# Later scatters, one block of scores and the first tile's rows taken forward, and a third 512-column first layer, in a fused attention and expert kernel

## The chip, the core and the metric

The kernel runs on one core of a Trainium2 chip, on five engines: TensorE (PE), whose weight loads are shown apart as PEld, VectorE (DVE), ScalarE (ACT), GpSimd (POOL) and SyncE (SP). SP and POOL issue DMA transfers. The metric is the device time of one launch in microseconds (us), the median of three runs; lower is better.

## The reference

Two layers follow one another. The first is a linear attention with a decay for each head, over 4 batches, 8 heads, 768 tokens and 64 channels; it goes through the tokens in blocks and carries a state of 64 by 64 per head.

```python
for b in range(nb):
    intra = np.einsum('bhic,bhjc->bhij', qb, kb) * Dmask[None]
    intra = np.einsum('bhij,bhjd->bhid', intra, vb)
    inter = np.einsum('bhid,bhde->bhie', qb * lam_pow[None], kv_state)
    out[:, :, sl] = intra + inter
    kv_state = lam_block[None, :, None, None] * kv_state + np.einsum('bhsd,bhse->bhde', kb_dec, vb)
```

Its output, 3072 tokens of 512 numbers, goes into a mixture of 8 experts. A token takes the one expert with the largest logit, and the expert is two layers of 512 by 1024 and 1024 by 512 with a ReLU between them.

```python
logits = x @ w_gate + modality_bias[modality_id]
e_idx = np.argmax(logits, axis=1)
for e in range(E):
    mask = e_idx == e
    h = np.maximum(x[mask] @ w1[e], 0.0)
    out[mask] = gate_w[mask, None] * (h @ w2[e])
```

## The kernel before

**Attention.** Tokens are taken in 24 blocks of 128 (`g` in the code), six to a batch, two to a step `m` (0 to 11). A block has scores (`scores`, L261, PE into the PSUM tile `s`, two buffers), the decay mask on DVE (`mask`, L267, into `pt`), decayed keys on ACT (`keys`, L243), decayed queries on POOL (`query`, L228, `qd`), the products that make the state (`products`, L275, PE into the single PSUM tile `kv`), the state's sum on DVE (`add`, L286), what comes from the state (`from_state`, L309) and from the block itself (`values`, L319), both PE into the PSUM tile `o` (two buffers), and a copy `xt` out of PSUM (`give`, L298). `block(g)` is scores, mask, keys and query. The loop over `m` works one step ahead: step m issues the blocks 2m+2 and 2m+3, then takes `from_state` and `values` of 2m and 2m+1, then the products of the next two.

**Rows.** After each odd step, `turns` turns four finished blocks from columns into rows by transposes on PE (`turn`, L338, into `o`), with the gate's logits between them (`gates`, L356). DVE (L345) and ACT (L348) copy each turned block from `o` into the rows `grp`.

**Routing.** Blocks are routed in three batches of 8. Small DVE operations work out a slot for each token; they are queued by `put` and issued a few at a time by `do(n)`. POOL then writes the rows to the DRAM tensor `placed`, block by block, with an indirect DMA (`one_slot`, L442 and L443). These scatters wait in a list of jobs; `tick(mm)` takes the next of them and lets it wait for the matmul mm. Those of the first batch go out in steps 5 to 7. A list of tiles is made of the counts: `early_list` "A" names the first two tiles of 256 tokens of one expert, "B" the next two, `late_list` the rest.

**Experts.** All products are made of float32 numbers split in a high part in fp32r and a low part, and a product is high by high, high by low and low by high. `fetch_x(n)` has SP fetch a tile's rows from `placed` (`xg`, four transfers of 128 KB, L629) and its tags (`idx`), after reading the place from a list by a register load; `fetch_w1` (`raw1`, L681) and `fetch_w2` (`raw2`, L685) fetch the weights in four parts of 512 KB. `turn_rows` transposes the rows on DVE in two halves (`turned`, L690, into `xt2`); `split_rows` and `split_w1` cast to high parts on ACT (L610, `xhl`, `w1h`) and subtract on DVE (L611, `xhl`, `w1l`); `low_w1` (L915) is such a subtraction for the first tile, into `low`. The first layer comes in two forms. `first_layer` makes three matmuls of 256 columns per piece (`three`, L702 to L704) into `s` and `kv` in turn, then a ReLU on ACT (`hh`, L725) and the low part on DVE (`hl`, L726). `first_joined` makes one matmul of 512 columns (high weights by high and low rows side by side, L742) and one of 256 (L741, L745) into `s`; then ACT copies one half (`hb`, L749), DVE adds the halves (`hs`, L751), ACT makes `hh` (L752) and DVE `hl` (L754). `second(n, t)` is the second layer of half a tile: 24 matmuls of 512 columns, a scaled copy on ACT (`y`, L769) and an indirect DMA on POOL to the output (L770). Before the change tiles 0 and 2 use `first_layer`, tile 1 and all from 3 on `first_joined`.

**Order.** PE, DVE, ACT and SP run in the order in which the code issues; POOL's order is made by dependencies that `pool` adds, which comes to the order of the code as well. So a transpose that waits for rows holds up all that DVE has behind it, and a fetch that waits holds up SP's later fetches. The attention's last steps, m = 9 to 11, overlap the first tile's preparation: in step 10 DVE turns the first tile's rows, and in step 11 it makes `xhl` and `low`. When the rows of tile 3 have been used, SP clears the end of each expert's region in `placed` (`clear_end`, eight transfers), then fetches w1 and the rows of `wides`, the fifth full tile (number 6 in the list).

Of the kernel before, what the change touches and what calls it, by code (L numbers as in the profile page):

```python
# [15 lines left out]
P = 128  # L16
# [27 lines left out]
def linear_attention_moe(tc, qkv, lam, modality, wg, mbias, w1, w2, out):  # L44
    nc = tc.nc
    with ExitStack() as ctx:
# [199 lines left out]
        scs = {}  # L246
# [110 lines left out]
                                          start=(p == 0), stop=(p == NP - 1), tile_position=(0, t * Q))  # L357
            return mm

        def turns(grp, amid):  # L360
            turn(grp, 0)
            turn(grp, 1)
            mm = gates(grp)
            do(4)
            amid()
            turn(grp, 2)
            return mm, turn(grp, 3)

        shape = [P, RC, E]

# [11 lines left out]
        def do(n=None):  # L382
            for what, args, kw in todo[:n]:
                what(*args, **kw)
            del todo[:n]
# [302 lines left out]
        def turned(out, rows):  # L688

            return nc.vector.transpose(out=out.rearrange("q p (t a) -> q t p a", a=Q),  # L690
                                       in_=rows.rearrange("q t (p a) -> q t p a", a=Q))

        def turn_rows(n):
            for h in range(2):
                turned(xt2[:, :, h * P : (h + 1) * P], xgs[n][:, 4 * h : 4 * (h + 1), :])

        def split_rows():
            for i in range(2):
# [126 lines left out]
        xgs = {}  # L825
# [30 lines left out]

        pairs = B * NC // HB
        def block(g, on_pool=False):
            mm = scores(g)
            mask(g)  # L860
            keys(g, on_pool)
            query(g)
            return mm
# [62 lines left out]
        for m in range(2, pairs):  # L926
            a, b = HB * m, HB * m + 1
            ahead = m + 1 < pairs
            add(b)
            if m == 4 or m == 8:  # L930
                routed = m // 4 - 1, *choose(m // 4 - 1, gate_rows())
            if ahead:
                block(a + 2)
                mm = block(b + 2)
                if m > 4:
                    tick(mm)
                if 2 < m <= pairs - SLOTS:
                    after(load(m + SLOTS - 1, [1]), mm)
                if m == 9:
                    fetch_w1(*some, parts=range(2, 4))  # L940
                elif m == 10:
                    fetch_w2(*some, parts=range(2, 4))
# [3 lines left out]
            if m == 10:  # L946
                w1h = w1_part("w1h", F32R, True)
                w1l0 = [work.tile([P, KC, TT], F32R, name="low", tag=f"both{i}" if i < 4 else "dk", bufs=1) for i in range(1, 5)]
                nc.scalar.copy(out=w1h[0], in_=raw1[0])
                do(4)  # L950
                turn_rows(0)
            elif not ahead:
                split_rows()
                low_w1(0)
                split(raw1[1], w1h[1], w1l0[1])
                do(4)
            elif m == 2:
                routing_constants()
            elif m == 3:
                clear(slice(E * CAP, E * CAP + TT), TT)  # L960
# [12 lines left out]
                mm = values(b)  # L973
            if m == 4 or m == 8:
                do(1)
            if m > 4:
                tick(mm)
            if m + SLOTS < pairs:
                load(m + SLOTS, [0])
            if ahead:  # L980
                mm = products(a + 2)
                mm = products(b + 2) or mm
                if m == 7:
                    tick(mm)
                add(a + 2)
            if m % 2 and ahead:
                ends = turns(m // 2, begin_list)
                if m == 5 or m == 9:
                    jobs += [("slots", one_slot)] * RC
                for mm in ends[: 2 if m % 4 == 1 else 1] if m > 4 else ():  # L990
                    tick(mm)
            if m == 8:
                need("slots")
# [74 lines left out]
            second(1, t)  # L1068
        need("slots")

        first_layer(amid2)
        fetch_w2(*fetch_regs(3))
        turn_rows(3)
        split_rows()
# [1 line left out]
        for e in range(E):  # L1076
            clear_end(e)
        do()
        fetch_w1(*fetch_regs(wides, True))
        fetch_x(wides)  # L1080
        for t in range(2):
            second(2, t)

# [114 lines left out]
```

## Time and profile before

| what | us |
|---|---|
| median of three runs | 383.61 |
| lowest and highest run | 383.05, 384.69 |
| the profiled execution, its own time | 384.85 |
| its span, first to last instruction | 383.1 |
| PE busy | 373.5 (97% of the span) |
| DVE busy | 282.9 (74%) |
| ACT busy | 237.4 (62%) |
| POOL busy | 99.0 (26%) |

The granted clock of TensorE was 0.997 over the span. Busy time of PE includes the overlap of neighbouring matmuls, whose ends are modelled: a stretch without idle time is a stretch in which starts follow each other, and the pace is read from the distance of starts, not from the length of one. An engine's idle time in brackets stands before an instruction, with what ended it. Times in the timelines are from the span's start.

### The profile page before, as it was taken

Reading aid. Unit: us, or ns where it says so; the run is one execution under the profiler, and the core shown is the slowest. Engines: PE = TensorE matmul, PEld = TensorE weight load, DVE = VectorE, ACT = ScalarE, POOL = GpSimd, SP = SyncE. Lnnn points to the kernel's source line nnn. Section 1 sums busy time; section 2 is a strip of 40 time slices with the busy share of each in tenths; the row PEclk is TensorE's granted clock in tenths of the full one; section 3 lists DMA queues with packets and bytes.
Section 4 is the critical chain, followed back from the end, with each engine's and each line's share of the span. In section 5 each row is a group of like instructions: output and inputs, shape, how many; then the busy total and the mean of one; then the engine's idle time right before and its main releaser. Section 6 shows DMA issues by size and latency. Waiting matters only on the chain.

```text
span 383.1 us, 9168 instructions
## 1 busy us (share of the span) xinstructions
PE 373.5 (97%) x3316; PEld 318.1 (83%) x3316; DVE 282.9 (74%) x506; ACT 237.4 (62%) x458; POOL 99.0 (26%) x130
## 2 busy tenths in 40 slices
PE   8999999999999999999999999999999999999993
PEld 3889989888998889888888877788878888888882
DVE  6677978779777889867789584486876868688630
ACT  1577676777766765564766664456566665776621
POOL 3653238628600177020100102102011020201112
PEclk9999999999999999999999999999999999999998
DMA  7999988999979684599714899763870210300100
GB/s 246 386 408 385 363 315 282 394 294 354 295 255 292 230 232 180 220 347 326 208 52 122 268 409 313 285 191 91 290 233 30 56 55 19 93 0 3 55 29 27
DMA packets 44597, 82.69 MB, mean 216 GB/s; under 512 B 7406, under 2 KB 20222, under 8 KB 44544
## 3 DMA queue, kind: packets, MB, share of 16 engines
q1 hardware_dynamic: 40592, 69.23, 55.6%
q0 software_dynamic: 3952, 12.79, 8.8%
q8 instruction: 28, 0.46, 0.5%
q14 instruction: 25, 0.20, 0.2%
HBM read 89.52 MB, written 17.85 MB: 280 GB/s over the span
## 4 chain that ended last, share of the span: by engine, by line
PE 56%; issue 33%; POOL 5%; DVE 3%; DMA 2%; SPq 0%; POOLq 0%; ACT 0%; DVEq 0%
PE s L742 8%; PE o L702 6%; PE o L704 6%; PE o L703 6%; PE s L261 6%; PE o L319 5%; POOL out_dram L770 4%; PE o L338 3%; PE s L741 3%; PE o L309 3%; PE kv L275 2%; DMA load<-in_qkv_dram 2%; PE x L356 1%; PE s L704 1%; PE kv L702 1%
## 5 line engine op out<-in xcount | busy, mean ns | idle before, releaser
L742 PE MATMUL s<-xhl,w1h 128*128 128x512 f32 x320 | 108.2, 395 | 0.0
L770 POOL DMA_INDIRECT out_dram<-y,idx x24 | 28.7, 1198 | 213.1 <-ACT y L769 167.8
L702 PE MATMUL o<-w2h,hh 128*128 128x512 f32 x192 | 75.1, 391 | 0.0
L703 PE MATMUL o<-w2l,hh 128*128 128x512 f32 x192 | 74.8, 389 | 0.0
L704 PE MATMUL o<-w2h,hl 128*128 128x512 f32 x192 | 74.7, 389 | 0.0
L741 PE MATMUL s<-xhl,w1l 128*128 128x256 f32 x240 | 67.2, 280 | 0.0
L742 PEld LDWEIGHTS s<-xhl,w1h 128*128 128x128 f32 x320 | 55.2, 188 | 7.7 <-issue 0.4
L751 DVE TENSOR_TENSOR hs<-s,hb 128x512 f32<-128x512 f32 x40 | 27.6, 690 | 43.8 <-ACT hb L749 43.8
L611 DVE TENSOR_TENSOR w1l<-raw,w1h 128x1024 fp32r<-128x1024 f32 x44 | 51.7, 1220 | 2.0 <-ACT w1h L610 2.0
L753 DVE TENSOR_TENSOR w2l<-raw,w2h 128x1024 fp32r<-128x1024 f32 x40 | 48.6, 1215 | 0.0
L741 PEld LDWEIGHTS s<-xhl,w1l 128*128 128x128 f32 x240 | 45.1, 188 | 3.6
L610 ACT CAST w1h<-raw 128x1024 fp32r<-128x1024 f32 x47 | 46.0, 1045 | 0.0
L752 ACT ACTIVATE hh<-hs 128x512 fp32r<-128x512 f32 x40 | 25.3, 633 | 30.7 <-DVE hs L751 29.9
L702 PEld LDWEIGHTS o<-w2h,hh 128*128 128x128 f32 x192 | 36.0, 188 | 7.8 <-issue 0.8
L704 PEld LDWEIGHTS o<-w2h,hl 128*128 128x128 f32 x192 | 36.0, 188 | 7.6
L703 PEld LDWEIGHTS o<-w2l,hh 128*128 128x128 f32 x192 | 36.1, 188 | 7.3
L735 ACT CAST w2h<-raw 128x1024 fp32r<-128x1024 f32 x40 | 41.5, 1038 | 0.0
L243 ACT ACTIVATE kd<-load,dk 128x64 f32<-128x64 f32 x144 | 35.7, 336 | 2.4 <-DMA load<-in_qkv_dram 2.3
L610 ACT CAST xhl<-xt 128x512 fp32r<-128x512 f32 x24 | 13.7, 619 | 30.9 <-DVE xt L690 29.7
L443 POOL DMA_INDIRECT placed<-grp,sloti x24 | 26.7, 1114 | 20.5 <-PE o L338 8.2
L228 POOL TENSOR_TENSOR qd<-load,pq 128x512 f32<-128x512 f32 x20 | 25.3, 1280 | 24.5 <-PE s L261 20.2
L267 DVE TENSOR_TENSOR pt<-s,dk 128x1024 f32<-128x1024 f32 x24 | 28.5, 1213 | 3.0 <-PE s L261 2.9
(209 smaller groups left out, 584.9 us busy)
## 6 DMA issues: line engine op xcount, KB each, us to landing
raw<-in_w_dram SPq DMA_DIRECT2D x96, 512.0 KB
load<-in_qkv_dram SPq DMA_DIRECT2D x12, 1024.0 KB
both<-in_w_dram SPq DMA_DIRECT2D x16, 512.0 KB
xg<-placed SPq DMA_DIRECT2D x48, 128.0 KB
placed<-blank SPq DMA_DIRECT2D x9, 528.0 KB
load<-in_qkv_dram SPq DMA_DIRECT2D x8, 512.0 KB
load<-in_qkv_dram SPq DMA_DIRECT2D x2, 2048.0 KB
load<-in_qkv_dram SPq DMA_DIRECT2D x4, 768.0 KB
```

The lines of the kernel that those rows point to most:

```text
L243: nc.scalar.activation(out=kds[g][:, p, hl, :], in_=kn[:, p, hl, :], func=AF.Copy, scale=dk[:, hl, p, P - 1 : P])
L267: nc.vector.tensor_tensor(out=pts[g], in0=scs.pop(g), in1=dk, op=ALU.mult)
L610: nc.scalar.copy(out=hi, in_=src)
L611: nc.vector.tensor_tensor(out=lo, in0=src, in1=hi.bitcast(F32), op=ALU.subtract)
L702: nc.tensor.matmul(out, ah, bh, start=first, stop=False)
L703: nc.tensor.matmul(out, ah, bl, start=False, stop=False)
L704: return nc.tensor.matmul(out, al, bh, start=False, stop=last)
L735: nc.scalar.copy(out=w2h[i], in_=raw2[i])
L741: nc.tensor.matmul(hp[:, j, :TT], w1l[i][:, kc, fs], xh[c][:, d, :], start=False, stop=False)
L742: mm = nc.tensor.matmul(hp[:, j, :], w1h[i][:, kc, fs], xhl[c][:, d].rearrange("p h t -> p (h t)"), start=(kc == 0), stop=(kc == KC - 1))
L753: nc.vector.tensor_tensor(out=w2l[i], in0=raw2[i], in1=w2h[i].bitcast(F32), op=ALU.subtract)
L770: sc = nc.gpsimd.indirect_dma_start(out=out, out_offset=bass.IndirectOffsetOnAxis(ap=idx[:, t, 0:1], axis=0), in_=y, in_offset=None, bound ...
```

## The change

Five things change. (1) The scatters of the first batch go out by other ticks: step 6 releases one (after its products) where it released two, step 7 one after the scores of block 16, one after the products and two after the turns, and the eighth is left to step 8, after the scores of block 19. (2) The scores of block 18 are issued in step 7 ahead of `turns`, and not at the head of step 8. (3) The first tile's rows are turned in step 9, a half between `gates` and the third turn and a half after the fourth, and not in step 10; in step 10 the state's sum of block 21 comes after the masks of blocks 22 and 23, `low_w1(0)` is issued there, and the four first operations of list B go from step 10 to step 11, behind the other part of `low`. (4) Tile 2's first layer is `first_joined`. (5) The rows of `wides` are fetched ahead of its w1.

```diff
--- before.py
+++ after.py
@@ -357,14 +357,17 @@
                                           start=(p == 0), stop=(p == NP - 1), tile_position=(0, t * Q))
             return mm
 
-        def turns(grp, amid):
+        def turns(grp, amid, rows=lambda h: None):
             turn(grp, 0)
             turn(grp, 1)
             mm = gates(grp)
             do(4)
             amid()
+            rows(0)
             turn(grp, 2)
-            return mm, turn(grp, 3)
+            last = turn(grp, 3)
+            rows(1)
+            return mm, last
 
         shape = [P, RC, E]
 
@@ -690,9 +693,12 @@
             return nc.vector.transpose(out=out.rearrange("q p (t a) -> q t p a", a=Q),
                                        in_=rows.rearrange("q t (p a) -> q t p a", a=Q))
 
+        def turn_half(n, h):
+            turned(xt2[:, :, h * P : (h + 1) * P], xgs[n][:, 4 * h : 4 * (h + 1), :])
+
         def turn_rows(n):
             for h in range(2):
-                turned(xt2[:, :, h * P : (h + 1) * P], xgs[n][:, 4 * h : 4 * (h + 1), :])
+                turn_half(n, h)
 
         def split_rows():
             for i in range(2):
@@ -856,7 +862,7 @@
 
         pairs = B * NC // HB
         def block(g, on_pool=False):
-            mm = scores(g)
+            mm = None if g in scs else scores(g)
             mask(g)
             keys(g, on_pool)
             query(g)
@@ -926,13 +932,18 @@
         for m in range(2, pairs):
             a, b = HB * m, HB * m + 1
             ahead = m + 1 < pairs
-            add(b)
+            if m != 10:
+                add(b)
             if m == 4 or m == 8:
                 routed = m // 4 - 1, *choose(m // 4 - 1, gate_rows())
             if ahead:
+                if m == 7:
+                    tick(scores(a + 2))
                 block(a + 2)
                 mm = block(b + 2)
-                if m > 4:
+                if m == 10:
+                    add(b)
+                if m == 5 or m > 7:
                     tick(mm)
                 if 2 < m <= pairs - SLOTS:
                     after(load(m + SLOTS - 1, [1]), mm)
@@ -947,13 +958,11 @@
                 w1h = w1_part("w1h", F32R, True)
                 w1l0 = [work.tile([P, KC, TT], F32R, name="low", tag=f"both{i}" if i < 4 else "dk", bufs=1) for i in range(1, 5)]
                 nc.scalar.copy(out=w1h[0], in_=raw1[0])
-                do(4)
-                turn_rows(0)
+                low_w1(0)
             elif not ahead:
                 split_rows()
-                low_w1(0)
                 split(raw1[1], w1h[1], w1l0[1])
-                do(4)
+                do(8)
             elif m == 2:
                 routing_constants()
             elif m == 3:
@@ -973,21 +982,23 @@
                 mm = values(b)
             if m == 4 or m == 8:
                 do(1)
-            if m > 4:
+            if m == 5 or m > 7:
                 tick(mm)
             if m + SLOTS < pairs:
                 load(m + SLOTS, [0])
             if ahead:
                 mm = products(a + 2)
                 mm = products(b + 2) or mm
-                if m == 7:
+                if m == 6 or m == 7:
                     tick(mm)
                 add(a + 2)
+                if m == 7:
+                    scores(a + 4)
             if m % 2 and ahead:
-                ends = turns(m // 2, begin_list)
+                ends = turns(m // 2, begin_list, (lambda h: turn_half(0, h)) if m == 9 else lambda h: None)
                 if m == 5 or m == 9:
                     jobs += [("slots", one_slot)] * RC
-                for mm in ends[: 2 if m % 4 == 1 else 1] if m > 4 else ():
+                for mm in ends if m > 4 else ():
                     tick(mm)
             if m == 8:
                 need("slots")
@@ -1068,7 +1079,7 @@
             second(1, t)
         need("slots")
 
-        first_layer(amid2)
+        first_joined(amid2)
         fetch_w2(*fetch_regs(3))
         turn_rows(3)
         split_rows()
@@ -1076,8 +1087,8 @@
         for e in range(E):
             clear_end(e)
         do()
+        fetch_x(wides)
         fetch_w1(*fetch_regs(wides, True))
-        fetch_x(wides)
         for t in range(2):
             second(2, t)
 
```

On DVE, in steps 9 to 11, this stands in a row before (`sloti` ends the second batch's slots, `grp` rows, `pt` masks, `geB` to `baseB` are of list B):

```order
L384 TENSOR_TENSOR sloti<-slot,m8s 128x8
L345 COPY grp<-o 64x512 x2
L286 SCALAR_TENSOR_TENSOR state_126<-state_125,pq,kv 128x64 x4
L267 TENSOR_TENSOR pt<-s,dk 128x1024 x2
L384 TENSOR_TENSOR geB<-x,thr 128x104
L384 TENSOR_REDUCE ntB<-geB 128x8
L384 MEMSET baseB 128x1
L384 TENSOR_TENSOR baseB<-ebase,nA 128x8
L690 STREAM_TRANSPOSE xt_132<-xg 128x4x4x32 x2
L286 SCALAR_TENSOR_TENSOR state_127<-state_126,pq,kv 128x64 x4
```

and this in the changed kernel, from the same operation on:

```order
L387 TENSOR_TENSOR sloti<-slot,m8s 128x8
L693 STREAM_TRANSPOSE xt_132<-xg 128x4x4x32
L345 COPY grp<-o 64x512 x2
L693 STREAM_TRANSPOSE xt_132<-xg 128x4x4x32
L267 TENSOR_TENSOR pt<-s,dk 128x1024 x2
L286 SCALAR_TENSOR_TENSOR state_126<-state_125,pq,kv 128x64 x4
L921 TENSOR_TENSOR low<-raw_1405,w1h 128x1024
L286 SCALAR_TENSOR_TENSOR state_127<-state_126,pq,kv 128x64 x4
L614 TENSOR_TENSOR xhl_133<-xt_132,xhl_133 128x2x256
L614 TENSOR_TENSOR xhl_134<-xt_132,xhl_134 128x2x256
L614 TENSOR_TENSOR low<-raw_1405,w1h 128x1024
L387 TENSOR_TENSOR geB<-x,thr 128x104
```

The transposes stand ahead of and behind the two row copies of the third and fourth turn, and the list's operations behind both parts of `low`.

On POOL, at the end of the first batch's scatters (L443; `qd` of blocks 19, 20 and 21), this stands before:

```order
L442 COPY grp_415<-pay_112 128x16
L443 DMA placed_117<-grp_415,sloti_895 26880x528
L228 TENSOR_TENSOR qd_1340<-load_943,pq_99 128x512
L228 TENSOR_TENSOR qd_1457<-load_1118,pq_99 128x512
L228 TENSOR_TENSOR qd_1479<-load_1118,pq_99 128x512
```

and this after:

```order
L228 TENSOR_TENSOR qd_1338<-load_943,pq_99 128x512
L445 COPY grp_415<-pay_112 128x16
L446 DMA placed_117<-grp_415,sloti_895 26880x528
L228 TENSOR_TENSOR qd_1457<-load_1114,pq_99 128x512
L228 TENSOR_TENSOR qd_1479<-load_1114,pq_99 128x512
```

The eighth scatter, the last that the first tile's rows wait for, has gone behind the queries of block 19, which wait for that block's scores.

On SP, behind the last of the eight clearings (`placed<-blank`), this stands before (`raw` is w1 here):

```order
L647 DMA placed<-blank 128x2x528
L673 TENSOR_LOAD listC
L673 ISA x2
L681 ISA
L681 DMA raw_1405<-in_w_dram 128x1024
```

and this after:

```order
L650 DMA placed<-blank 128x2x528
L628 TENSOR_LOAD listC
L628 ISA x2
L1142 TENSOR_LOAD nums
L1142 ISA x2
L632 ISA
L632 DMA xg<-placed 32x8x128
```

The rows' four transfers now come right behind the clearings, with a register load of `nums` (the number of tiles) that stood at the end of SP's program before, and the four parts of w1 come behind them.

## Rows read from the trace of the kernel before

**Rows 1.** The page, part 1, and one group of part 5 (busy, mean ns | idle).
```profile
PE 373.5 (97%) x3316; PEld 318.1 (83%) x3316; DVE 282.9 (74%) x506; ACT 237.4 (62%) x458; POOL 99.0 (26%) x130
...
L751 DVE TENSOR_TENSOR hs<-s,hb 128x512 f32<-128x512 f32 x40 | 27.6, 690 | 43.8 <-ACT hb L749 43.8
```

**Rows 2.** Windows: length, busy time and count of PE, PEld, DVE, ACT, POOL.
```profile
60.00:80.00 20.00, 19.37 (x385) 17.39 (x381) 16.35 (x49) 15.01 (x54) 13.31 (x18) 1.00 1.01 360
80.00:100.00 20.00, 18.77 (x339) 16.99 (x339) 17.91 (x45) 13.17 (x32) 11.93 (x15) 1.00 1.07 315
```

**Rows 3.** Timeline of PE, steps 7 and 11: start, length, what [idle before].
```profile
67.54 1.09 PE L338 MATMUL o<-ident,xt 128*128 128x128 f32 x8 [0.23 <-ACT xt L298]
...
69.91 1.23 PE L338 MATMUL o<-ident,xt 128*128 128x128 f32 x8 [0.27 <-DVE grp L345]
...
96.05 0.38 PE L704 MATMUL s<-xhl,low 128*128 128x256 f32 x1 [1.23 <-DVE low L915]
...
98.76 1.04 PE L338 MATMUL o<-ident,xt 128*128 128x128 f32 x8
```

**Rows 4.** Timeline of DVE from the third turn of step 9 on.
```profile
85.82 1.28 DVE L345 COPY grp<-o 64x512 f32<-64x512 f32 x2 [0.48 <-PE o L338]
87.03 0.84 DVE L286 SCALAR_TENSOR_TENSOR state<-state,pq,kv 128x64 f32<-128x64 f32 x4
87.79 2.34 DVE L267 TENSOR_TENSOR pt<-s,dk 128x1024 f32<-128x1024 f32 x2
90.05 0.25 DVE L384 TENSOR_TENSOR geB<-x,thr 128x104 f32<-128x104 f32 x1
...
90.52 1.14 DVE L384 TENSOR_TENSOR baseB<-ebase,nA 128x8 f32<-128x8 f32 x1
...
91.59 1.29 DVE L690 STREAM_TRANSPOSE xt<-xg 128x512 f32<-128x512 f32 x2
92.81 0.81 DVE L286 SCALAR_TENSOR_TENSOR state<-state,pq,kv 128x64 f32<-128x64 f32 x4
93.57 1.29 DVE L611 TENSOR_TENSOR xhl<-xt,xhl 128x512 fp32r<-128x512 f32 x2
94.78 1.22 DVE L915 TENSOR_TENSOR low<-raw,w1h 128x1024 fp32r<-128x1024 f32 x1
...
97.05 0.15 DVE L384 TENSOR_TENSOR ntB<-ntB,nA 128x8 f32<-128x8 f32 x1
...
97.56 0.67 DVE L298 COPY xt<-o 128x512 f32<-128x512 f32 x1
```

**Rows 5.** Timeline of POOL: the first batch's eighth scatter, then queries.
```profile
71.92 0.99 POOL L443 DMA_INDIRECT placed<-grp,sloti  x1 [0.52 <-issue]
73.37 1.27 POOL L228 TENSOR_TENSOR qd<-load,pq 128x512 f32<-128x512 f32 x1 [0.47 <-PE s L261]
...
89.12 2.52 POOL L228 TENSOR_TENSOR qd<-load,pq 128x512 f32<-128x512 f32 x2
```

**Rows 6.** Timeline of SP's DMA queue: start of the first issue, length of all.
```profile
78.09 2.36 SPq L629 DMA_DIRECT2D xg<-placed  x4
...
169.21 2.13 SPq L681 DMA_DIRECT2D raw<-in_w_dram  x4
172.18 2.30 SPq L629 DMA_DIRECT2D xg<-placed  x4
```

**Rows 7.** DMA views: POOL's queue in 77 to 78; all packets in 80.6 to 85.3.
```profile
q0 software_dynamic: 5, 0.01, 3.2%
...
DMA packets 1489, 1.03 MB, mean 218 GB/s; under 512 B 348, under 2 KB 1372, under 8 KB 1486
```

**Rows 8.** Windows: the first layers of tile 2 and tile 3, columns as in rows 2.
```profile
143.66:155.06 11.40, 11.40 (x98) 11.39 (x97) 10.97 (x29) 6.24 (x8) 7.84 (x9) 1.00 0.49 182
165.97:177.16 11.19, 11.19 (x65) 9.79 (x64) 7.77 (x10) 7.54 (x11) 1.33 (x2) 1.00 0.98 358
```

**Rows 9.** Timeline of DVE: tile 2's last `hl`; the transposes of `wides`.
```profile
156.38 0.68 DVE L726 SCALAR_TENSOR_TENSOR hl<-kv,hh 128x512 fp32r<-128x512 f32 x1
...
181.96 1.31 DVE L690 STREAM_TRANSPOSE xt<-xg 128x512 f32<-128x512 f32 x2 [1.48 <-DMA xg<-placed]
```

## The prediction

> **What bounds the kernel now.** I read the cores' view and the page first. PE is busy for 97% of the span, the other engines for 74% and less [rows 1]: the kernel is as long as PE's work and PE's idle time. So the second view is the windows, to see where PE idles after its start. Between 60 and 80 it lacks 0.63, between 80 and 100 it lacks 1.23 [rows 2]; from there to the last tiles its windows are full, and the tail behind them isn't touched by the change. Third, PE's timeline shows what ended those waits [rows 3]: 0.23 and 0.27 in the turns of step 7 (the copy `xt`, then the row copies) and 1.23 in the first tile's first layer, whose third matmul needed `low` from DVE. All idle time that the change can take away is thus 0.23 + 0.27 + 1.23 = 1.73. Last, I followed DVE ahead of that `low` [rows 4]: masks, a list operation of 8 columns that took 1.14, two transposes of the first tile's rows, a state's sum, `xhl`, `low`, one straight after the other.
>
> **Part 1 and 2, the scatters and the scores.** The scores of block 18 stand between PE's last products and its turns in step 7, so PE has a block's work while `xt` and then the row copies are made. The same 16 matmuls leave step 8. Worth 0.5 (0.23 + 0.27), if nothing later eats it. The price is on POOL. Before, the eighth scatter started at 71.92, ahead of the queries of block 19, which waited for that block's scores and ran from 73.37 to 74.64 [rows 5]. Now it stands behind them. With PE 0.5 ahead the queries end at 74.1; a tag copy and a pause (0.52 in the bracket of the scatter's row, and about 0.2, an estimate from there) put the scatter at 74.9, 3.0 later.
>
> **Part 3, the first tile's rows.** SP fetched them at 78.09 [rows 6], 6.2 after the eighth scatter's start; POOL's queue still moved five packets of it between 77 and 78 [rows 7], so the fetch went out as the scatter landed. Scatter later by 3.0: fetch at 81.1. Before, the four transfers, 1024 packets counted under 2 KB and over 512 B (1372 less 348), moved between 80.6 and 85.3 [rows 7]: 4.7 long, and 2.5 behind the issue, as two parts of w1 are ahead of them in the queue. Those parts get a start of 3.0 now, so the wait behind them lies between 0 and 2.5. The rows are there at X = 81.1 + 4.7 + (0 to 2.5), 85.8 to 88.3; I take the middle, X = 87.0, as no row is nearer to either end. The ends for the scatter itself: no later than before, X = 85.3; or as long from issue to the end as the fetch itself took (7.2 in place of 6.2), X = 89.3.
>
> DVE comes to the first transpose at about 85, somewhat ahead of the time at which the third turn's copies stood (85.82), and waits until X. Behind it, in its new order and with the durations from start to start [rows 4]: half of the rows 0.61, two row copies 1.21, the other half 0.61, two masks 2.26, a sum 0.76, `low` 1.14, a sum 0.76, `xhl` 1.21, `low` 1.14, eight list operations 1.13 (0.47 and 0.15 for the four that come from step 10, without the long one's 1.14; 0.51 for the other four). That is 10.83; then the copy `xt` of the last block takes 0.67, and with 0.1 to reach PE the next turn can start at X + 11.6. Before it started at 98.76 [rows 3]. At X = 87.0 it starts at 98.6: **0.2 gained**. So the wait for `low` goes (both sums and `low` come before PE asks), but most of it and the 0.5 from step 7 come back as DVE's wait for rows, with PE held by the row copies and then by `xt`.
>
> The long list operation ran to 91.66, which is where POOL's queries ended (89.12 + 2.52) [rows 4, 5]. The Trainium skill (SBUF — State Buffer, "Who interferes with whom") says that a DVE instruction with two SBUF inputs is kept out while GpSimd reads SBUF; the row agrees. By that rule the moved `low` would be blocked too if it came before 91.6; at X = 87.0 it comes at 92.4, behind the queries, and the sum stays as it is.
>
> **Part 4, tile 2.** The same columns in fewer matmuls: 11.40 in three of 256, 11.19 in a 512 and a 256 [rows 8]: **0.21 gained**. The page TensorE: Matmul & The Clock Gate of the Trainium skill ("Back-to-back issue gap") gives about 131 ns for a sustained matmul of 512 columns. That would make some 3 us of this part, as an estimate by that page; rows 8 give 0.35 for a 512 and a 256 together, and the row decides.
>
> Against it, DVE gets four `hs` of 0.69 more [rows 1] where it was already busy for 10.97 of 11.40 [rows 8]: 13.7 of work for 11.2 of time, 2.5 behind. Its last `hl` was ready at 157.06 [rows 9] and will be at 159.5. PE asks for it in the 21st matmul of the second layer; at 0.227 each (10.91 between the first layers in rows 8, by 48) that is 143.66 + 11.19 + 4.55 = 159.4. So 0.1 is lost. The backlog then runs into tile 3's preparation and first layer, where DVE is busy for only 7.77 of 11.19 [rows 8]: nothing. **0.1 gained** in all; bounds 0.2 gained and, if DVE is 1.0 later than reckoned, 0.8 lost.
>
> **Part 5, rows ahead of w1.** Before, w1 of `wides` was issued at 169.21 and its rows at 172.18 [rows 6], and the transposes waited until 181.96, 1.48 of it idle [rows 9]; PE did not idle there, so freeing the rows is worth nothing. Now SP holds w1 until the rows' transfers are out, and these may not pass the clearings; if they go out no earlier than before, w1 is issued at about 176, 7 later. Its casts come after the transposes anyway, 183.3 before, and that cover is about 7. Cost nothing, and, where the cover fails, what w1 is late by. The load of `nums` on SP waits for DVE's last list operation, which is ready before the clearings end.
>
> **Sum.** 0.2 + 0.1 = 0.3. Against the profiled execution's own 384.85 (span 383.1, 1.75 around it) that is 384.55. The runs' median is 383.61, 1.2 under it; I subtract from the median: **383.3**.
>
> **Rivals.** (a) The rows are early: X at or below 85. Then PE's own work sets the end, and all 1.73 goes, with 0.1 of tile 2: 381.8. For it: the fetch finds an emptier queue. Against it: the scatter is 3.0 later. By the rule on the shared port the `low` would then stand at about 90.2 and be blocked to 91.1; DVE would give 1.5 instead of 1.73, 382.0.
> (b) The rows are late, and the kernel is **slower**. One mechanism: a transpose that waits in the middle of step 9's turns blocks the row copies behind it, these block `o`, and PE stops. It decides from X = 87.2, and each us of X costs one. At X = 89.3 the turn comes at 100.9, 2.1 late: 385.6 with tile 2's 0.1. For it: the fetch already waited for the scatter before. Against it: w1's parts no longer stand ahead.
> (c) DVE's backlog in tile 2 is larger: 0.8 lost there, 384.2.
> (d) Part 4 doesn't do what it says because PE is paced by columns: 0.2 at most, already in the sum.
>
> **How the numbers follow.** Chances: about no change (X from 86 to 88) 0.55, early 0.15, late 0.18, backlog 0.12. The range that should hold 8 in 10 goes from 381.8 (early) to 385.6 (late). A measurement of this kernel can tell about 0.5%, 1.9, from no change. Early alone reaches 1.8 and passes 1.9 only if tile 2 gives its full 0.2, so faster by more than that has 0.10. Slower by more than that needs X over 89.1: most of (b), 0.15. Within it: 0.75.
>
> **What would show it.** Right: idle of DVE ahead of the first transpose in step 9, ended by the rows, of 1 to 3; no wait of PE for `low` any more; in its place PE idle ahead of `from_state` of step 10 (row copies) or of the turn behind the first piece (`xt`); no idle of PE at step 7's turns; tile 2's first layer 11.2 long, with the second layer waiting 0 to 0.3 for the last `hl`. Wrong: rows that land before DVE asks, or a fetch that goes out at 78 as before (early), PE idle of over 2 in step 10 (late), PE idle around 188 (w1 of `wides` late).

## The result, and the profile after

The changed kernel takes 387.97 us (median of six runs, 387.41 to 389.86), the kernel before 383.62 (383.05 to 384.69): 1.0122 times as long (95%: 1.0093 to 1.0151), **1.2% slower**. The prediction was 383.3 and a range of 381.8 to 385.6: about no change was forecast, and the time lies above the range. It is the side of rival (b), the late rows, and longer than (b) reckoned.

The profiled execution took 387.41 with a span of 385.7, before 384.85 and 383.1. So the two traces have 2.56 of the 4.35 between the medians. The other 1.8 is in no row: the execution profiled before was 1.23 above its median, the one after 0.56 below its own. The two longest executions of the changed kernel (389.5 and 389.86) had a mean granted clock of 0.990, the other four 0.993 or 0.994; in which stretch isn't recorded.

The windows of the kernel after (length, PE busy and count, PEld, DVE, ACT, POOL, granted clock, DMA share, GB/s), to be read beside [rows 2]; the third is the stretch of low clock:

```profile
60.00:80.00 20.00, 20.00 (x400) 18.24 (x397) 18.89 (x50) 15.07 (x55) 13.95 (x18) 1.00 1.00 370
80.00:100.00 20.00, 16.99 (x294) 15.19 (x291) 14.02 (x40) 11.75 (x29) 9.55 (x13) 0.91 0.79 236
90.38:93.79 3.41, 3.41 (x42) 2.71 (x42) 3.41 (x6) 0.00 (x0) 1.61 (x4) 0.50 1.01 392
```

Between 60 and 80 PE has no idle time left: the 0.63 of before is gone, as forecast. Between 80 and 100 it lacks 3.01 for 1.23, and the granted clock, 1.00 all through this stretch before, is 0.91. PE's timeline (start, length, what, [idle before and what ended it]), beside [rows 3]:

```profile
67.77 1.09 PE L338 MATMUL o<-ident,xt 128*128 128x128 f32 x8
...
69.81 1.09 PE L338 MATMUL o<-ident,xt 128*128 128x128 f32 x8
...
90.24 2.57 PE L309 MATMUL o<-qd,state 64*64 64x128 f32 x32 [3.00 <-DVE grp L345]
92.74 2.46 PE L319 MATMUL o<-pt,load 128*64 128x128 f32 x32
...
98.38 0.38 PE L708 MATMUL s<-xhl,w1h 128*128 128x256 f32 x1
...
101.31 1.04 PE L338 MATMUL o<-ident,xt 128*128 128x128 f32 x8
```

Step 7's turns have no bracket any more, nor has the first tile's first layer: both waits went. In their place stands one of 3.00 ahead of `from_state` of step 10, ended by a row copy, and behind it `from_state` takes 2.57 and the values 2.46. The turn of step 11 starts at 101.31, 2.55 later than before. DVE's timeline, beside [rows 4]:

```profile
88.81 0.71 DVE L693 STREAM_TRANSPOSE xt<-xg 128x512 f32<-128x512 f32 x1 [4.44 <-DMA xg<-placed]
89.45 1.24 DVE L345 COPY grp<-o 64x512 f32<-64x512 f32 x2
90.62 0.68 DVE L693 STREAM_TRANSPOSE xt<-xg 128x512 f32<-128x512 f32 x1
...
97.85 1.23 DVE L614 TENSOR_TENSOR low<-raw,w1h 128x1024 fp32r<-128x1024 f32 x1
...
100.04 0.68 DVE L298 COPY xt<-o 128x512 f32<-128x512 f32 x1
```

DVE waited 4.44 for the rows, the row copies came behind them at 89.45, and PE had its `o` at 90.24. Why the rows were late is in POOL's timeline, in the list of DMA issues of 75.0 to 75.9 (engine, operation, count, us from issue to landing), and in the timeline of SP's queue, beside [rows 5, 6]:

```profile
72.43 0.99 POOL L446 DMA_INDIRECT placed<-grp,sloti  x1 [0.52 <-ACT kd L243]
73.45 1.29 POOL L228 TENSOR_TENSOR qd<-load,pq 128x512 f32<-128x512 f32 x1
...
75.40 1.03 POOL L446 DMA_INDIRECT placed<-grp,sloti  x1 [0.52 <-POOL grp L445]
```
```profile
placed<-grp,sloti POOLq DMA_INDIRECT x1, 7.4
```
```profile
75.13 0.93 SPq L684 DMA_DIRECT2D raw<-in_w_dram  x2
82.84 2.36 SPq L632 DMA_DIRECT2D xg<-placed  x4
```

The eighth scatter started at 75.40 (before 71.92), landed 7.4 later, and the fetch went out right then, at 82.84 (before 78.09). The rows were there 5.97 after that. The query ahead of the scatter did not start with its block's scores: it has no bracket and follows the seventh scatter (72.43 and 0.99), so POOL's own queue set its start.

The row of SP's queue at 75.13 is the first two parts of w1, 1 MB, 0.27 ahead of the scatter; before, they went out at 76.27, 4.35 behind it. From 79 to 80 this queue took 94.4% of the DMA engines' time and the scatters' 6.2%, with 6 packets; from 80 to 81 the scatters moved 62.

The third tile's first layer (first window) and what follows up to the fourth's (second), then PE in the second one and DVE's `hl`, beside [rows 8, 9]:

```profile
146.21:157.40 11.19, 11.19 (x65) 9.78 (x64) 10.53 (x28) 6.32 (x9) 7.70 (x9) 1.00 0.51 187
157.40:168.87 11.47, 11.37 (x50) 8.93 (x49) 10.43 (x24) 7.48 (x10) 0.00 (x0) 1.00 0.46 173
```
```profile
161.81 0.50 PE L709 MATMUL o<-w2l,hh 128*128 128x512 f32 x1
162.41 0.50 PE L710 MATMUL o<-w2h,hl 128*128 128x512 f32 x1
```
```profile
161.67 0.68 DVE L760 SCALAR_TENSOR_TENSOR hl<-hs,hh 128x512 fp32r<-128x512 f32 x1
```

11.19 for 11.40 as forecast, but 11.47 for 10.91 behind it: the last `hl` ends at 162.35, and PE's next matmul that reads it starts 0.60 after the one ahead of it, where 0.23 is the mean of the second layer before. So the account of the two traces is: 2.55 to the turn of step 11, 0.21 gained and 0.56 lost at the third tile, nothing in the fifth tile, and 0.3 given back from the fourth tile to the end (216.8 for 217.1): 2.6.

### The profile page after: what moved, and what is told of

The parts are those of the page before. It is cut to its first block, busy times and chain, and to the rows that moved or that the text cites. A ratio compares the mean times of both kernels' runs of the same rounds, so it can differ in the third digit from the quotient of the medians.

```text
span 385.7 us, 9102 instructions
## 1 busy us (share of the span) xinstructions
PE 375.1 (97%) x3284; PEld 317.9 (82%) x3284; DVE 286.4 (74%) x510; ACT 239.4 (62%) x462; POOL 98.4 (26%) x130
## 4 chain that ended last, share of the span: by engine, by line
issue 34%; PE 33%; DMA 11%; DVE 8%; POOL 6%; ACT 4%; SPq 1%; POOLq 0%; DVEq 0%
DMA load<-in_qkv_dram 6%; PE s L748 6%; POOL out_dram L776 4%; PE o L319 4%; DMA xg<-placed 3%; PE o L710 3%; PE o L708 3%; PE o L709 3%; PE s L261 3%; PE o L309 2%; PE s L747 2%; DVE w2l L759 2%; DMA placed<-grp,sloti 2%; DVE w1l L614 2%; PE o L338 1%
## 5 line engine op out<-in xcount | busy, mean ns | idle before, releaser
L748 PE MATMUL s<-xhl,w1h 128*128 128x512 f32 x352 | 118.9, 395 | 0.0
L709 PE MATMUL o<-w2l,hh 128*128 128x512 f32 x192 | 74.9, 390 | 0.0
L747 PE MATMUL s<-xhl,w1l 128*128 128x256 f32 x264 | 73.9, 280 | 0.0
L748 PEld LDWEIGHTS s<-xhl,w1h 128*128 128x128 f32 x352 | 60.7, 188 | 8.5 <-issue 0.4
L757 DVE TENSOR_TENSOR hs<-s,hb 128x512 f32<-128x512 f32 x44 | 30.3, 689 | 42.2 <-ACT hb L755 42.2
L759 DVE TENSOR_TENSOR w2l<-raw,w2h 128x1024 fp32r<-128x1024 f32 x44 | 53.4, 1214 | 0.0
L747 PEld LDWEIGHTS s<-xhl,w1l 128*128 128x128 f32 x264 | 49.6, 188 | 4.0
L758 ACT ACTIVATE hh<-hs 128x512 fp32r<-128x512 f32 x44 | 27.8, 633 | 35.2 <-DVE hs L757 35.2
L741 ACT CAST w2h<-raw 128x1024 fp32r<-128x1024 f32 x44 | 45.6, 1037 | 0.0
L446 POOL DMA_INDIRECT placed<-grp,sloti x24 | 27.7, 1154 | 26.8 <-PE o L338 9.7
L755 ACT COPY hb<-s 128x512 f32<-128x512 f32 x44 | 25.5, 578 | 13.9 <-PE s L748 12.8
```

The costliest lines, as they stand in the source:

```text
L709: nc.tensor.matmul(out, ah, bl, start=False, stop=False)
L741: nc.scalar.copy(out=w2h[i], in_=raw2[i])
L747: nc.tensor.matmul(hp[:, j, :TT], w1l[i][:, kc, fs], xh[c][:, d, :], start=False, stop=False)
L748: mm = nc.tensor.matmul(hp[:, j, :], w1h[i][:, kc, fs], xhl[c][:, d].rearrange("p h t -> p (h t)"), start=(kc == 0), stop=(kc == KC - 1))
L757: nc.vector.tensor_tensor(out=hs, in0=hp[:, :, :TT], in1=hb, op=ALU.add)
L759: nc.vector.tensor_tensor(out=w2l[i], in0=raw2[i], in1=w2h[i].bitcast(F32), op=ALU.subtract)
```

## Experiments

**Theory A**: the late scatter and the early transposes together make the loss; DVE waits for rows, PE for the row copies, and the idle PE then runs at half clock. **Rivals**: the scatters' new places cost by themselves; the early transposes cost by themselves; the loss sits in the third or the fifth tile. Each comparison has its own runs of the kernel before on its chip; that kernel's median lay between 385.09 and 385.43 there, so ratios are compared, not times.

### The rows in step 10 again

```diff
                 low_w1(0)
+                turn_rows(0)
...
-                ends = turns(m // 2, begin_list, (lambda h: turn_half(0, h)) if m == 9 else lambda h: None)
+                ends = turns(m // 2, begin_list)
```


> The changed kernel with one thing undone: both transposes of the first tile's rows stand in step 10 again, behind the subtraction `low` for the first part of w1, and not among the turns of step 9. Theory A (the transposes block the row copies behind them, PE stops for 3.0 and then runs at half clock): both go, since in step 9 nothing on DVE waits for the rows any more. The rows landed at 88.8 in the changed kernel, ahead of their place in step 10 (the masks alone end at about 91), so nothing waits for them at all. The scores' move keeps its 1.0 (the turns of step 9 at 82.1 for 83.1), and the wait for `low` (1.23 before) falls to 0.3 or less. Against the kernel before: 1.0 + 0.9 gained, 0.2 gained and 0.5 lost in the third tile: 382.0, between 381.5 and 383.0; PE has no idle time of over 0.5 between 85 and 100 and its clock stays at 1.0. Theory B (the loss sits in the scatters' places, in the third tile or in the fifth tile's fetch): 386 or more, the rows' place being worth under 1.

Measured: 385.72 for 385.35, ratio 1.0005 (0.9988 to 1.0022). The loss of 1.2% is gone with this one edit, and no low clock is left ahead of the tail: theory A holds. But 382.0, half a per cent faster, did not come. What PE and DVE did (timelines):

```profile
93.96 1.09 PE L309 MATMUL o<-qd,state 64*64 64x128 f32 x28 [0.43 <-DVE state L286]
```
```profile
90.50 1.94 DVE L921 TENSOR_TENSOR low<-raw,w1h 128x1024 fp32r<-128x1024 f32 x1
```

PE waits for the state's sum, which stands behind the rows, which stand behind a `low` that takes 1.94 for 1.2. A second wait, of 0.82, stands ahead of the turn of step 11, which starts at 98.89: the copy `xt` comes behind the other `low` and the list's operations. The first `low` started while POOL's queries were running, to 91.34. That is what the prediction feared by the page SBUF — State Buffer of the Trainium skill ("Who interferes with whom", DVE's second port pair is shared with GpSimd and locked); the row agrees: 91.34 plus 1.1 is its end, 92.44.

### The wait filled with matmuls

```diff
+                if m == 10:
+                    for i in range(14):
+                        nc.tensor.matmul(small_ps[:, 384:], ident, ident, start=True, stop=True)
                 from_state((a, b))
```


> The changed kernel with 14 matmuls more on PE, of the identity by itself into a part of PSUM that nothing reads, between the scores of blocks 22 and 23 and from_state of step 10, that is in the stretch in which PE waited for the row copies. The wait for the rows on DVE stays as it was. Theory A1 (the clock fell because PE idled for 3.0, and it cost 1.5 in from_state and 0.5 in the values): the clock stays at 1.0, from_state takes 1.1 and the values 2.0, as before the change. DVE's chain, which does not hang on TensorE's clock, then sets the time: the last subtraction for the first layer ends at about 97.7 and the turn of step 11 comes 11.6 behind the rows. So of the 2.0 only 0.9 to 1.4 come back: 386.2 to 386.8 where the changed kernel has 387.4. Theory A2 (the clock fell for another reason, whatever PE does in the wait): from_state still takes 2.5 and the time is that of the changed kernel, 387 to 388. If the matmuls take over 3.0 they cost what is over.

Measured: 388.51 for 385.35, ratio 1.0072 (1.0045 to 1.0099). PE's timeline, DVE's first transpose and its copy `xt`, and the window from the added matmuls to the values:

```profile
88.17 3.39 PE L982 MATMUL x<-ident 128*128 128x128 f32 x28
92.56 0.44 PE L309 MATMUL o<-qd,state 64*64 64x128 f32 x4 [1.00 <-DVE grp L345]
93.16 1.09 PE L309 MATMUL o<-qd,state 64*64 64x128 f32 x28 [0.16 <-DVE grp L345]
...
96.77 0.69 PE L275 MATMUL kv<-load,kd 128*64 128x64 f32 x16 [0.63 <-DVE state L286]
```
```profile
91.13 0.71 DVE L693 STREAM_TRANSPOSE xt<-xg 128x512 f32<-128x512 f32 x1 [6.20 <-DMA xg<-placed]
...
101.94 0.68 DVE L298 COPY xt<-o 128x512 f32<-128x512 f32 x1
```
```profile
88.17:94.20 6.03, 4.87 (x64) 4.32 (x62) 3.07 (x5) 1.84 (x5) 4.63 (x6) 1.00 0.94 309
```

The rows came later still in this execution (the fetch went out at 84.81, ahead of the added matmuls, so they are not its cause), yet the clock stayed at 1.00: it was the idle PE that had lost it (A1). With the clock kept, the turn of step 11 starts at 103.13, 12.0 behind the rows; in the changed kernel it starts 12.5 behind them. So of the 2.0 that `from_state` and the values took longer at half clock, 0.5 reached the turn: the rest took the place of PE's waits for DVE, 0.16 and 0.63 here, which the changed kernel doesn't have behind its 3.00. The copy `xt` ended at 102.62, 11.5 behind the rows, and the turn started 0.5 after that: PE still had its own work to do, in a row since the products at 96.77, which had waited for the state's sum. The time's own gain is not shown: this ratio's interval overlaps the next one's.

### The changed kernel once more

> The changed kernel itself once more, as the measure for the others on the same chip, since the kernel before alone has moved from 383.6 to 385.4 between the first comparison and the second. Both theories: 1.2% over the kernel before, with the rows landing 3 or more behind DVE's ask, PE idle for about 3 ahead of from_state of step 10, and the clock at half for some us behind that. If the clock does not fall in the profiled execution while PE idles as long, the fall is not the idle time's alone.

Measured: 389.79 for 385.43, ratio 1.0109 (1.0073 to 1.0145). Transposes at 89.73, PE idle for 2.98, the clock at 0.5 from 92.08 for 3.41, the turn of step 11 at 102.46, 12.7 behind the rows: the same picture.

### Part 3 alone

The kernel before, and of the diff only `turns` with `rows`, the rows' place, `add(b)`, `low_w1(0)` and the list operations.

> The kernel before with part 3 alone: the first tile's rows are turned among step 9's turns, but the scatters and scores stand as before. Theory A1 (the scatter's lateness is what makes the rows late): the eighth scatter starts at 71.9, the rows are there at 85.9, DVE waits for 0 to 1.5 at the first transpose, the turn of step 11 comes 11.6 behind the rows, at 97.5 for 98.8: 0.3% faster. Theory A2 (the rows' place in step 9 is too early for any fetch of this kernel): DVE waits for 3 or more, PE idles for 2 or more in step 10, 0.3% slower or more. The measure that tells them apart is the start of the transposes.

Measured: 385.84 for 385.43, ratio 1.0004 (0.9983 to 1.0026). Timelines of POOL, DVE and PE:

```profile
71.89 0.98 POOL L446 DMA_INDIRECT placed<-grp,sloti  x1 [0.52 <-issue]
```
```profile
86.11 0.71 DVE L693 STREAM_TRANSPOSE xt<-xg 128x512 f32<-128x512 f32 x1 [0.66 <-DMA xg<-placed]
```
```profile
88.25 1.10 PE L309 MATMUL o<-qd,state 64*64 64x128 f32 x32
...
98.21 1.04 PE L338 MATMUL o<-ident,xt 128*128 128x128 f32 x8
```

With the scatter at 71.89 the rows are there at 86.11, DVE waits 0.66 and PE's `from_state` not at all: A1. The turn is 12.1 behind the rows, 0.55 earlier than before the change. That gain is below what the comparison can tell.

### Parts 1 and 2 alone

The kernel before with the new ticks and with `scores(a + 4)` in step 7; the rows stay in step 10.

> The kernel before with parts 1 and 2 alone: scores of block 18 ahead of step 7's turns, the scatters on the new hooks, and the rows still turned in step 10. The prediction: 0.5 gained at step 7's turns and nothing lost, as the rows (there at 88 to 89) are ahead of their place in step 10 (91.6): 0.1% faster at best. What was seen of the changed kernel in other executions: the turns of step 9 begin at 82.1 in one and at 83.0 in another, for 83.1 before, so the gain lies between 0 and 1.0, and the wait for `low` at the first layer stays or grows: 0.1% faster to 0.1% slower. Theory B, that the late scatter costs time even where the rows are turned in step 10: 0.3% slower or more.

Measured: 384.65 for 385.09, ratio 0.9990 (0.9971 to 1.0009). The late scatter costs nothing where the rows are turned in step 10. PE still waits for `low`:

```profile
95.63 0.39 PE L704 MATMUL s<-xhl,low 128*128 128x256 f32 x1 [1.23 <-DVE low L915]
```

So neither half loses anything alone; with both, and with parts 4 and 5, the kernel loses 1.1 to 1.2%. Parts 4 and 5 without the others cost nothing (0.9988, below).

### The scatters one tick earlier, twice

```diff
-            if m == 5 or m > 7:
+            if m == 5 or m == 6 or m > 7:
                 tick(mm)
             if m + SLOTS < pairs:
```


> The changed kernel with one hook more for a scatter, at the values of step 6, so that every later scatter of the first batch moves up by one hook and the eighth stands ahead of the queries of block 18. Theory A1: the eighth scatter starts at about 73 for 75.4, its fetch goes out at about 80 for 82.8, the rows are there at 86, the wait of PE ahead of from_state of step 10 falls from 3.0 to under 0.7, the clock stays at 1.0, and the kernel gains 2.5 or more over the changed one: 0 to 0.3% faster than the kernel before. Theory A2 (the rows' landing does not hang on the eighth scatter): as the changed kernel, 1.2% slower.

> The changed kernel with the earlier scatters once more, on the same chip as the one without part 4, with more rounds: 0.2 to 0.3% faster than the kernel before, that is 1.3% under the changed kernel. If the first comparison was chance: no difference to the kernel before.

Measured: 384.66 for 385.43, ratio 0.9974 (0.9952 to 0.9995), and the second time 386.13 for 385.09, 1.0024 (1.0003 to 1.0045). DVE's first transposes, in the first and in the second:

```profile
86.75 0.71 DVE L693 STREAM_TRANSPOSE xt<-xg 128x512 f32<-128x512 f32 x1 [1.46 <-DMA xg<-placed]
```
```profile
87.73 0.71 DVE L693 STREAM_TRANSPOSE xt<-xg 128x512 f32<-128x512 f32 x1 [1.81 <-DMA xg<-placed]
```

The eighth scatter starts at 73.08 and 74.11, the rows follow, and by the ratios 0.8 to 1.5% is gained on the changed kernel: A1. Whether it beats the kernel before stays open, the two comparisons disagree. In the second, `from_state` of step 6 took 2.7 (63.20 to 65.87) in place of 1.0, in short stops for which the profile names no cause; three scatters stand in POOL there in a row.

### Parts 4 and 5

Part 4 alone (`first_joined(amid2)` for `first_layer(amid2)` in the kernel before), part 5 alone (`fetch_x(wides)` ahead of `fetch_w1`), and both.

> The kernel before with part 4 alone: the third tile's first layer in 512-column matmuls. The prediction's reckoning: 0.21 gained in the first layer, 0.1 lost in the second, 383.5. By the changed kernel's trace: 0.21 gained, 0.56 lost behind it (second layer 11.47 for 10.91), so 0.35 slower, 384.0. Rival: the loss in that trace belongs to the later scatters or lists and not to this part, 383.4. All are within 0.5% of the kernel before; what tells them apart are the two stretches in the trace (first layer 11.19, and 10.9 or 11.5 up to the next).

> The kernel before with part 5 alone: the rows of the fifth tile fetched ahead of its w1. The prediction: no change, 383.6, since the casts of w1 come behind the transposes anyway (183.3) and DVE's wait there (1.48) cost PE nothing; w1 issued some 7 later. Rival: w1 is late, PE idles at about 188 and the kernel is slower by that; in the changed kernel's trace PE had no such wait, but all stood 2.9 later there. The time tells them apart at 0.5% or more, the trace below that.

> The kernel before with parts 4 and 5 together, and nothing of parts 1 to 3. Part 4 alone cost 0.47%: DVE's backlog ran into the last list, so the clearings, w1 and the rows of the fifth tile came 2 to 4 later and PE idled for 2.5 at 188, after which the clock fell. Theory A (part 5 is the cover for part 4: with the rows ahead of w1 the transposes start as soon as they did before): the idle time at 188 goes, and the time is that of the kernel before, within 0.2%, that is 0.2 gained in the first layer and up to 0.6 lost in the second. Theory B (part 5 does nothing, as predicted, and w1 is late in any case): 0.4 to 0.6% slower, with PE idle at 188.

Measured: part 4 alone 387.30, ratio 1.0047 (1.0027 to 1.0066); part 5 alone 385.68, 1.0009 (0.9985 to 1.0034), both for 385.35; the two together 385.23 for 385.43, 0.9988 (0.9967 to 1.0010). None of the expectations for part 4 alone had 0.5%. Its trace, SP's queue, DVE, PE, and a window:

```profile
171.67 2.94 SPq L681 DMA_DIRECT2D raw<-in_w_dram  x4
175.45 2.50 SPq L629 DMA_DIRECT2D xg<-placed  x4
```
```profile
186.14 1.30 DVE L690 STREAM_TRANSPOSE xt<-xg 128x512 f32<-128x512 f32 x2 [5.50 <-DMA xg<-placed]
```
```profile
189.62 0.51 PE L742 MATMUL s<-xhl,w1h 128*128 128x512 f32 x1 [1.29 <-ACT w1h L610]
190.88 0.39 PE L745 MATMUL s<-xhl,w1l 128*128 128x256 f32 x1 [0.76 <-DVE w1l L611]
```
```profile
192.09:195.50 3.41, 3.41 (x12) 2.84 (x12) 2.14 (x2) 2.85 (x5) 1.69 (x2) 0.50 0.20 33
```

DVE's backlog delays the last list's operations, with them the clearings (159.96 for 157.38), and with these the fifth tile's w1 (171.67 for 169.21) and rows (175.45 for 172.18 in [rows 6]). The transposes slip from 181.96 to 186.14, PE idles for 2.05 at 189 to 191, and from 192.09 the clock is 0.50 for 3.41. With part 5 as well (SP, DVE, PE):

```profile
175.29 1.95 SPq L629 DMA_DIRECT2D xg<-placed  x4
```
```profile
180.57 1.30 DVE L690 STREAM_TRANSPOSE xt<-xg 128x512 f32<-128x512 f32 x2
```
```profile
188.21 0.40 PE L742 MATMUL s<-xhl,w1h 128*128 128x512 f32 x1
```

The rows go out no earlier, but with nothing ahead of them in the queue they land in time, and the wait is gone. Part 5 is part 4's cover, worth 0.6% beside it and nothing without it. In both traces the second layer up to the fourth tile takes 11.2, not the 11.47 of the changed kernel: of the 0.56 lost there, 0.27 is part 4's own, and the other 0.3 comes only with the other parts; which of them brings it isn't shown.

### The earlier scatters without part 4

The tick of above, and `first_layer(amid2)` again.

> The changed kernel with the earlier scatters and without part 4: the third tile's first layer in 256-column matmuls again. From the traces: with part 4 the stretch from the third tile's first layer to the fourth's takes 22.8 (143.64 to 166.41), without it 22.3 (143.66 to 165.97 in the kernel before), so 0.46 comes back. Theory A (part 4 is a loss of its own, paid in the second layer that waits for `hl`): 0.1% faster than the next kernel, 0.3 to 0.4% faster than the kernel before, about 384.2 where that has 385.4. Rival (what is lost there is given back before the fifth tile, by the rows that are ahead of w1): as the next kernel.

Measured: 385.49 for 385.09, ratio 1.0009 (0.9987 to 1.0031), beside 1.0024 (1.0003 to 1.0045) with part 4. From the third tile's first layer to the fourth's its trace takes 22.31, with part 4 22.68. The sign fits theory A; the intervals overlap, and 0.3 to 0.4% faster than the kernel before did not come.

### The list behind `low`, the rows left in step 10

```diff
                 nc.scalar.copy(out=w1h[0], in_=raw1[0])
-                do(4)
                 turn_rows(0)
...
                 split(raw1[1], w1h[1], w1l0[1])
-                do(4)
+                do(8)
```
on top of parts 1 and 2.

> The kernel before with parts 1 and 2, and of part 3 only what does not hang on the rows: the four list operations that stood ahead of the first tile's transposes in step 10 (the long one of 1.14 among them) go behind both subtractions `low`. The rows are turned in step 10, where nothing waited for them. Theory A (the wait for `low`, 1.23 to 1.39 in every kernel that keeps that order, is DVE's backlog, and can be had without turning the rows earlier): `low` is ready 1.6 sooner, PE waits for 0 to 0.3 in the first tile's first layer, the turn of step 11 comes at about 97.0 for 98.3, and the kernel is 0.3 to 0.4% faster than the kernel before, about 384. Rival 1: the subtraction that now comes sooner stretches to 1.9, as it did in two kernels while POOL's queries ran, and the list operations press on the copy `xt` for the turn: half of it comes back, 0.1 to 0.2% faster. Rival 2: the later list makes the third tile's fetch late: no change or slower, with PE idle in front of tile 2.

Measured: 384.43 for 385.32, ratio 0.9971 (0.9951 to 0.9991): 0.3% faster than the kernel before in this one comparison, and 1.4 to 1.5% faster than the changed one by its two ratios. The earlier scatters showed as much in their first comparison and not in their second, so a gain in time on the kernel before isn't settled. The traces show where it would come from. DVE, PE, and the window of 80 to 100:

```profile
89.58 1.29 DVE L690 STREAM_TRANSPOSE xt<-xg 128x512 f32<-128x512 f32 x2
...
93.18 1.21 DVE L915 TENSOR_TENSOR low<-raw,w1h 128x1024 fp32r<-128x1024 f32 x1
```
```profile
94.45 0.39 PE L704 MATMUL s<-xhl,low 128*128 128x256 f32 x1
...
97.40 1.06 PE L338 MATMUL o<-ident,xt 128*128 128x128 f32 x8
```
```profile
80.00:100.00 20.00, 19.80 (x358) 17.82 (x355) 17.73 (x46) 14.30 (x36) 11.40 (x17) 1.00 0.81 256
```

`low` comes 1.2 earlier than with parts 1 and 2 alone, PE's wait for it falls from 1.23 to under 0.3, PE lacks 0.20 in the stretch, and the turn of step 11 stands at 97.40 for 98.33. The wait that part 3 was set against goes without turning the rows any earlier.

## Why the prediction was wrong

**What bounds the kernel**: right. All idle time it named went in the changed kernel (step 7's turns, and the wait for `low`); what was lost is idle time and clock of PE elsewhere.

**Parts 1 and 2**: the turns' gain was there. The scatter was put at 74.9 and started at 75.40, 0.5 of the miss: the prediction let block 19's query start earlier with PE, but POOL's seventh scatter held it until 73.42.

**Part 3, the step that failed** is the time from the scatter's start to the fetch: 6.2 was carried over from before, 7.4 was measured (1.2 of the miss). It isn't one execution's chance: the distance is 6.2 in all five traces with the scatter in its old place, 6.1 to 6.7 in the three with it one tick earlier, and 7.2 to 8.8 in all six with it behind block 19's query. The prediction had 7.2 as an end of its range and reckoned with 6.2. What lengthens it was not tested by itself. In those six traces w1's first two parts go out 0.25 to 0.27 ahead of the scatter, in the other eight 2.6 to 4.4 behind it; the prediction counted these parts only as standing ahead of the fetch, where their earlier start would help. POOL's next pair of queries also comes closer behind the scatter (1.8 for 4.6 or more), and no run parts the two. From the fetch to the rows it reckoned 5.9 and 5.97 was measured. So X was 88.8 and not 87.0. That is still inside the forecast's own end of 89.3 and would give 385.1 by its rule, inside its range; what lies above the range comes from the terms below, which the prediction left out or made too small.

**The chain behind X** was reckoned at 11.6. The kernels that kept the clock give 12.1, 12.0 and 12.0 (part 3 alone, the earlier scatter, the filled wait): 0.4 short. DVE's own part of it was right: in these three the copy `xt` starts 10.8 behind the rows, as reckoned, and ends at 11.5. But PE was not waiting for it. Behind the state's sum of block 21, which DVE makes earlier in that chain, PE has products, values, `from_state` and the first layer's first piece to do, 6.4 in the filled wait (96.77 to 103.13), and that path ends later. Its rule of 1 us per us of X held from 86.1 to 91.1.

**The clock** stood in no rival. PE idled for 3.0, and the clock was 0.50 for the next 3.41: the chain became 12.5, another 0.5. The row that could have warned was the forecast of (b) itself: it let PE stop for some us and priced only the stop. The Trainium skill has the rule (TensorE: Matmul & The Clock Gate, "HAM oscillation — how this bites in real kernels": a PE left waiting for data comes back at half clock); the traces agree, at 90.38 here, and the filled wait shows the reverse. With part 4 alone the clock fell at 192.09 behind stops of only 1.29 and 0.76, shorter than the waits that the section tells of. It changed the time and should have been weighed.

Together: 0.5 + 1.2 + 0.1 for X, 0.4 and 0.5 make 2.7, the distance from the 98.6 forecast for the turn to 101.31.

**Part 4**: the gain of 0.21 was right to the digit. "0.1 lost" was 0.56 in the changed kernel, inside the bound of 0.8 that the prediction gave, and 0.27 where part 4 stood without parts 1 to 3. "The backlog then runs into tile 3's preparation: nothing" was wrong: alone, part 4 costs 0.47%, through the list, the clearings and the fifth tile's rows.

**Part 5**: "worth nothing" was right for the kernel before (1.0009) and wrong beside part 4 (1.0047 without it, 0.9988 with it): the cover was reckoned from the lists' old times, and part 4 moved the lists.

**The sum** was set against a median that lay 1.23 under the profiled execution, and the range held nothing for that. With X as measured, the prediction's own rule gives 385.1 for (b); the chain, the clock and the third tile add 1.3, and the stretch from the fourth tile on gives 0.3 back. What then remains up to 387.97, 1.8, is the distance of the two profiled executions from their medians, and no trace shows where it lies.

## What to carry to other kernels

An instruction that waits for a transfer blocks everything its engine has behind it: before it is moved ahead, the transfer's latest landing has to be found, and when the same change also moves the transfer's producer later, the two moves are priced together, since here each was free and both cost 1.2%. Filler work of an engine's queue, such as list operations that nobody needs for a while, is the safer thing to move out of the way: it waits for nothing, and here PE's wait for `low` went with it. And a stop of TensorE of some us is priced as the stop and the slow stretch behind it.

## What the runs showed of the hardware

TensorE's granted clock fell from 1.00 to 0.50, that is from 2.4 to 1.2 GHz, behind idle times of 3.0 (twice, in the changed kernel) and behind 1.29 and 0.76 close together (part 4 alone), each time for 3.41; behind 1.00 ahead of which PE had been kept busy it did not. At half clock `from_state` took 2.57 for 1.10 and the values 2.46 for 1.97. The changed kernel's indirect scatters took from 3.1 to 7.4 from issue to landing, the eighth of the first batch 7.4. Short stops of PE in step 6, up to 1.6 in all and without a releaser, came and went between executions of kernels with the same order there; what causes them stays open.
